# A fused attention and gated-mixing kernel: all eight PSUM banks named by hand, and one written order for all engines

## The chip, the cores and the metric

The kernel runs on one core of a Trainium2 chip. The metric is the device time of one execution in microseconds (us). The core's engines are called by the names of the profile: PE (matrix multiplication, with PEld for its weight loads), DVE (vector work), ACT (activation functions and copies), POOL and SP (here they mostly issue transfers).

## The reference, cut to what matters

Four batches (B = 4) with eight heads (H = 8), a sequence of 768 and a head size of 64. First an attention in which a query sees the 96 keys up to itself and the first 8 keys, with a bias that grows with distance; then a gated mixing over tokens and channels.

```python
scores = scale * np.matmul(q, k.transpose(0, 1, 3, 2)) + bias     # bias = -slope[h] * distance
scores = np.where(is_global | is_local, scores, -1e9)
a = softmax(scores)
x = np.matmul(a, v)                        # to (B, 768, 512): heads side by side
theta = x @ w_theta
zr, zi = x * np.cos(theta), x * np.sin(theta)
y = einsum('ts,bsd->btd', w_tok_r, zr) + einsum('ts,bsd->btd', w_tok_i, zi)
u = x + y
out = u + np.maximum(u @ w_ch, 0.0)
```

## The kernel before, in words

Everything is cut into blocks of 128 tokens (NT = 6 of them) and pairs of heads (NP = 4). All matmuls take bf16. One batch goes through these steps:

- **q and k turned.** q and k of a head pair must lie with the head size on the partitions. Batch 0 is turned by 12 PE transposes of half width (`turn`, L221), batches 1 and 2 by 6 PE transposes (`prep`, L267) of a copy that DVE regroups (`prep_copy`, L252), batch 3 by DMA transposes on SP (`prep_dma`, L284). Copies bring the turned blocks out of PSUM (L232, L271, L273), and `kglob` (L241, L243) makes the copy of k whose first 8 columns are the global keys.
- **Scores.** `score_mms` (L325) makes a chunk of two token blocks for both heads of a pair: 8 matmuls (6 in the last chunk of three), each with 64 rows, the head size, and 128 columns. The two heads use the two halves of the PE array. In batch 0 the bias is first laid into PSUM by matmuls (`score_bias`, L298 and L305); in the others `score_exp` (L335) takes the exponential on ACT and DVE multiplies by a table (L344, L347), which `bias_table` (L148) made per head.
- **Values.** `values` (L387) makes 22 matmuls of 65 columns for a pair, the last column being the softmax sum; DVE divides (L392, L394). `xtrans` turns the result for the next product, by PE transposes (L405, L406) or by DMA transposes (L398).
- **Theta and sines.** `theta` (L428): 24 matmuls of 512 columns for a batch; `sines` on ACT (L438); DVE multiplies (L442) into `zri`.
- **Mix and channels.** `mix` (L453): for each of 6 token blocks 12 matmuls of 512 columns, in three groups of 4, then an addition on DVE (L458). `utrans` turns u, by PE and ACT (L471, L472) or by a DMA transpose (L467). `chan` (L481): 4 matmuls of 512 columns, a DVE instruction (L486) and the store (L488).
- **Token weights.** `trans_w` (L185 to L189) turns the token-mixing weights once, in 72 PE transposes.

PSUM is given out by two pools: `big`, two tiles of two banks each, for scores, values of batches 1 to 3 and theta; and `small`, four tiles of one bank, for all else. A pool hands out its tiles in turn.

The order has three parts. Up to `manual.close()`, batch 0's attention, its theta and its first mixes, the written order of the calls is the order of all engines. Then a loop over batches describes batch b's mix (`main`) and batch b+1's attention (`attention_steps`, as `side`), `weave` interleaves the two by weights, and the tile framework's scheduler makes the engines' queues from it, helped by some anchors (`behind`). The last four calls are in a manual order again, for PE and DVE. Loads go through POOL's queue in the order of `load_w` and what follows it.

```python
    big = ctx.enter_context(tc.tile_pool(name="big", bufs=2, space=bass.MemoryType.PSUM))
    small = ctx.enter_context(tc.tile_pool(name="small", bufs=4, space=bass.MemoryType.PSUM))
```

Of the kernel before, what the change touches and what calls it, by code (L numbers as in the profile page):

```python
# [16 lines left out]
def kernel(  # L17
# [32 lines left out]
    big = ctx.enter_context(tc.tile_pool(name="big", bufs=2, space=bass.MemoryType.PSUM))  # L50
    small = ctx.enter_context(tc.tile_pool(name="small", bufs=4, space=bass.MemoryType.PSUM))

    def ps_big():
        return big.tile([T, 2, 512], FP, name="pb", tag="pb")

    def ps_small(shape, dtype):
        return small.tile(shape, dtype, name="ps", tag="ps")


# [3 lines left out]
    def alloc_qk(b):  # L63
        loads[b] = [ld.tile([T, 2, H, NT, D], BF, name="qk"), None]

    def alloc_v(b):
        vn = loads[b][1] = ld.tile([T, H, NT, D + 1], BF, name="vn")
        nc.vector.memset(vn[:, :, :, D:D + 1], 1.0)
# [38 lines left out]
    alloc_v(0)  # L107
    load_qk(0, 2, 2)
# [51 lines left out]
    def load_w():  # L160
        def tok(tt, wis=(0, 1)):
            for wi, src in [(w_, (moe_w_tok_r, moe_w_tok_i)[w_]) for w_ in wis]:
                w2 = moe.tile([T, 2, S], BF, name="w_nat", bufs=6)
                nc.gpsimd.dma_start(
                    out=w2, in_=src[tt * T:(tt + 2) * T, :].rearrange("(a p) s -> p a s", p=T))
                w_nat[wi, tt], w_nat[wi, tt + 1] = w2[:, 0], w2[:, 1]
        def wth(lo, hi):
            nc.gpsimd.dma_start(out=w_theta_bf[:, lo:hi], in_=moe_w_theta.rearrange("(c p) n -> p c n", p=T)[:, lo:hi])
        tok(0)
        wth(0, 2)  # L170
        wth(2, 4)
        tok(2)
        load_all_qk(1)
        tok(4)
        nc.gpsimd.dma_start(out=w_ch_bf, in_=moe_w_ch.rearrange("(c p) n -> p c n", p=T))
        load_all_v(1)
        load_all_qk(2)

    def trans_w(tt, copy=nc.vector.tensor_copy, wide=False, copy0=nc.vector.tensor_copy):
        pb = big.tile([T, 2, 2 * 512], BF, name="pbw", tag="pb") if wide else None  # L180
        tiles = [pb[:, wi, 0:S].rearrange("p (t n) -> p t n", t=NT) if wide else ps_small([T, NT, T], BF)
                 for wi in range(2)]
        for wi, ps in enumerate(tiles):
            for st in range(NT):
                nc.tensor.transpose(ps[:, st, :], w_nat[wi, tt][:, st * T:(st + 1) * T], ident)  # L185
            if not wide:
                (copy if wi else copy0)(out=w_tokT[wi][:, :, tt * T:(tt + 1) * T], in_=ps)
        for wi, ps in enumerate(tiles if wide else ()):
            (copy if wi else copy0)(out=w_tokT[wi][:, :, tt * T:(tt + 1) * T], in_=ps)  # L189


    def warm(n):
        ps = ps_small([T, 512], FP)
        for _ in range(n):
            nc.tensor.matmul(ps, lhsT=zero[:, 0:T], rhs=zero, start=True, stop=True)


    x_sb, xT_sb = {}, {}
    qkT = {}

    anchor = {}

    def alloc_x(b):
        x_sb[b] = moe.tile([T, NP, NT, T], BF, name="x_sb", bufs=2)
        xT_sb[b] = moe.tile([T, NC, S], BF, name="xT", bufs=1)

    def behind(eng):

        return tc.issue_after(anchor[eng]) if eng in anchor else nullcontext()

    tiles0 = {}

    qk0 = att.tile([T, 2, 2, NT, D], BF, name="qk0", tag="qkn", bufs=2)

    def cast0(i_, eng, h):
        eng(out=qk0[:, i_, h], in_=qk32[:, i_, h])

    def turn(ps, src):
        for t_ in range(NT):
            for hh in range(2):  # L220
                nc.tensor.transpose(ps[hh * D:(hh + 1) * D, t_, :], src[:, hh, t_, :], ident)  # L221

    def turn0(p, i_):
        ps = tiles0[p, i_] = ps_small([T, NT, T], BF)
        turn(ps, loads[0][0][:, i_, 2 * p:2 * p + 2] if p else qk0[:, i_])

    def out0(p, i_, copy, half=None):
        to = qkT.setdefault((0, p), [None, None, None])
        if to[i_] is None:
            to[i_] = att.tile([T, S], BF, name=("qT", "kT")[i_], tag=("qT", "kT")[i_], bufs=6)  # L230
        ns = slice(0, T) if half is None else slice(half * T // 2, (half + 1) * T // 2)
        copy(out=to[i_].rearrange("p (n t) -> p n t", t=NT)[:, ns],  # L232
             in_=tiles0[p, i_].rearrange("p t n -> p n t")[:, ns])

    def kglob(b, p, t0=0, t1=NT - 2, copy=nc.vector.tensor_copy):
        kT = qkT[(b, p)][1]
        if t0 == 0:
            qkT[(b, p)][2] = att.tile([T, NT - 2, T], BF, name="kG", bufs=6)
        kG = qkT[(b, p)][2][:, t0:t1]
        with behind("zri" if p else "dve") if b == B - 1 else nullcontext():  # L240
            copy(  # L241
                out=kG, in_=kT[:, (t0 + 1) * T:(t1 + 1) * T].rearrange("p (t n) -> p t n", t=t1 - t0))
            copy(out=kG[:, :, 0:NG], in_=kT[:, None, 0:NG].to_broadcast([T, t1 - t0, NG]))  # L243

    qkns = {}

    def prep_copy(b, p):
        qk = loads[b][0]
        qkn = qkns[b, p] = att.tile([T, NT, 2, 2, D], BF, name="qkn", bufs=2)
        with behind("dve"):  # L250
            for i_ in range(2):
                nc.vector.tensor_copy(  # L252
                    out=qkn[:, :, i_].rearrange("p t h d -> p h t d"), in_=qk[:, i_, 2 * p:2 * p + 2])

    def prep(b, p):
        if p == 0 or (b, p) == (2, NP // 2):
            prep_copy(b, p)
        if p + 1 < NP and (b, p) != (2, NP // 2 - 1):
            prep_copy(b, p + 1)
        qkn = qkns[b, p]  # L260
        qT = att.tile([T, S], BF, name="qT", bufs=6)
        kT = att.tile([T, S], BF, name="kT", bufs=6)
        for i_, dst in ((0, qT), (1, kT)):
            ps = ps_small([T, NT, T], BF)
            with behind("pe"):
                for t_ in range(NT):
                    nc.tensor.transpose(ps[:, t_, :], qkn[:, t_, i_].rearrange("p h d -> p (h d)"), ident)  # L267
            dst = dst.rearrange("p (n t) -> p n t", t=NT)
            src = ps.rearrange("p t n -> p n t")
            if i_ == 0:  # L270
                nc.vector.tensor_copy(out=dst, in_=src)  # L271
            else:
                nc.scalar.copy(out=dst, in_=src)  # L273

        qkT[(b, p)] = [qT, kT, None]
        kglob(b, p)

    def prep_dma(b, p):
        qk = loads[b][0]
        qkT[(b, p)] = [None, None, None]  # L280
        for i_ in (1, 0):
            to = qkT[(b, p)][i_] = att.tile([T, S], BF, name=("qT", "kT")[i_], bufs=6)
            with behind("sp"):
                nc.sync.dma_start_transpose(  # L284
                    out=to.rearrange("p (t s) -> p t s", t=NT),
                    in_=qk[:, i_, 2 * p:2 * p + 2].rearrange("p h t d -> p (h t d)"))

    ebuf = {}

    pbs = {}  # L290

    def score_bias(p, c):
        pb = pbs[0, p, c] = ps_big()
        n = min(4, 2 * NT - 1 - 4 * c)
# [14 lines left out]
    def score_mms(b, p, c):  # L309
        qT, kT, kG = qkT[(b, p)]  # L310
        if c == 0:
            ebuf[(b, p)] = att.tile([T, 2, NT, 2, T], BF, name="e", bufs=3)
        if b:
            pbs[b, p, c] = ps_big()
        pb = pbs[b, p, c]
# [12 lines left out]
    def sine_table():  # L328
        nc.scalar.activation(junk, halfpi, AF.Sin)

    def score_exp(b, p, c):
        e_t, pb = ebuf[(b, p)], pbs[b, p, c]
        n = min(4, 2 * NT - 1 - 4 * c) * T
        e_c = e_t[:, :, 2 * c:2 * c + 2].rearrange("p a j s n -> p a (j s n)")[:, :, 0:n]
        ins = nc.scalar.activation(e_c, pb[:, :, 0:n], AF.Exp, scale=scale).ins  # L335
        if b and c == NT // 2 - 1 and p == NP - 1:
            with tc.issue_after(ins):
                sine_table()
        if b == 0:
            return  # L340
        tab = etab[:, 2 * p:2 * p + 2]
        if c == 0 or n < 4 * T:
            s0 = 0 if c == 0 else 2
            nc.vector.tensor_mul(e_c, e_c, tab[:, :, s0:s0 + n // T].rearrange("p a s n -> p a (s n)"))  # L344
        else:
            e4 = e_t[:, :, 2 * c:2 * c + 2].rearrange("p a j s n -> p a j (s n)")
            nc.vector.tensor_mul(  # L347
# [20 lines left out]
    def values(b, p, hh, i0=0, i1=NT):  # L368
# [20 lines left out]
        if b and hh == 0:  # L389
            return  # L390
# [348 lines left out]
```

## Time and profile before

| | us |
|---|---|
| median of 3 runs (lowest, highest) | 171.81 (171.68, 172.01) |
| the profiled execution's own time | 171.37 |
| its span, first to last instruction | 169.3 |
| PE, PEld busy | 158.8, 85.1 |
| DVE, ACT, POOL busy | 126.7, 104.6, 38.8 |

The profiled execution took 2.07 us more than its span: what lies before the first and behind the last instruction. Its own time is 0.44 us under the median of the runs.

By stages, with the first theta matmul of each batch as borders (a table by windows of the trace; busy us):

| window | what PE does in it | length | PE | DVE | ACT |
|---|---|---|---|---|---|
| 0 to 8.31 | warm-up, bias, first transposes | 8.31 | 5.77 | 5.80 | 4.64 |
| 8.31 to 24.28 | attention of batch 0 | 15.97 | 15.07 | 11.21 | 14.42 |
| 24.28 to 66.93 | theta and mix of 0, attention of 1 | 42.65 | 41.26 | 37.07 | 35.11 |
| 66.93 to 104.23 | theta and mix of 1, attention of 2 | 37.30 | 35.94 | 32.87 | 24.00 |
| 104.23 to 137.17 | theta and mix of 2, attention of 3 | 32.94 | 32.56 | 25.61 | 19.63 |
| 137.17 to 165.40 | theta and mix of 3, channels | 28.23 | 28.03 | 13.46 | 6.77 |
| 165.40 to 169.30 | last DVE instructions and stores | 3.90 | 0.15 | 0.67 | 0.00 |

How to read it: matmuls are pipelined, and the profile models their ends, so PE can show as busy while nothing enters it. Starts are exact. So the distance from one start to the next tells what a matmul costs in a stream.

### The profile page before, as it was taken

How to read it: one execution, taken by the hardware profiler on the slowest of the kernel's cores; microseconds unless marked ns; L12 is line 12 of the kernel's file. 1: busy time of each engine (PE TensorE's matmuls, PEld its weight loads, DVE VectorE, ACT ScalarE, POOL GpSimd, SP SyncE). 2: the span in 40 equal slices, each digit the busy share in tenths (PEclk: the TensorE clock that was granted, in tenths of full speed). 3: DMA queues.
4: the chain of work that ended last, by engine and by line, in shares of the span. 5: the costliest groups of instructions: out<-in, count | busy, mean ns of one | idle time of the engine just before them, and what ended most of it. 6: DMA issues, size and time to landing. Idle time of an engine off the chain costs nothing.

```text
span 169.3 us, 3778 instructions
## 1 busy us (share of the span) xinstructions
PE 158.8 (94%) x1546; PEld 85.1 (50%) x1569; DVE 126.7 (75%) x265; ACT 104.6 (62%) x134; POOL 38.8 (23%) x46
## 2 busy tenths in 40 slices
PE   7689989999989999999989999999999999999991
PEld 2346755557655455545545464444555544444440
DVE  6748877699999997989998697787877837614442
ACT  4698898995599694799842641999257109400010
POOL 8975439005164101049700000000000000000000
PEclk9999999999999999999999999999999999999999
DMA  5999999999999999709999895776137472233335
GB/s 152 204 172 180 209 206 205 203 209 180 152 202 220 149 172 162 146 6 200 137 125 127 211 166 135 134 149 217 35 77 143 111 170 96 95 62 93 93 96 183
DMA packets 72704, 25.34 MB, mean 150 GB/s; under 512 B 60784, under 2 KB 69744, under 8 KB 72688
## 3 DMA queue, kind: packets, MB, share of 16 engines
q0 software_dynamic: 45696, 12.45, 87.8%
q1 hardware_dynamic: 26576, 12.13, 32.5%
q10 hardware_dynamic: 416, 0.52, 0.9%
q8 instruction: 12, 0.20, 0.5%
q14 instruction: 4, 0.03, 0.1%
HBM read 25.69 MB, written 6.29 MB: 189 GB/s over the span
## 4 chain that ended last, share of the span: by engine, by line
PE 64%; DVE 16%; ACT 11%; DMA 4%; issue 2%; DVEq 0%; SPq 0%
PE ps L453 27%; PE ps L481 9%; PE pb L428 6%; PE pb L325 5%; ACT cs L438 4%; ACT e L335 4%; PE pb L387 4%; PE ps L428 3%; DMA qk<-in_k_dram 3%; PE ps L267 2%; DVE x_sb L394 2%; DVE e L344 2%; DMA xT<-x_sb 2%; PE ps L405 2%; DVE e L347 2%
## 5 line engine op out<-in xcount | busy, mean ns | idle before, releaser
L453 PE MATMUL ps<-zri,w_tokT 128*128 128x512 bf16 x272 | 67.8, 380 | 0.8 <-issue 0.2
L335 ACT ACTIVATE e<-pb 128x1024 bf16<-128x1024 f32 (+1 forms) x48 | 43.6, 955 | 16.6 <-PE pb L325 16.1
L453 PEld LDWEIGHTS <-w_tokT 128*128 128x128 bf16 x288 | 25.8, 98 | 27.3 <-DVE w_tokT L189 0.6
L458 DVE TENSOR_TENSOR u<-x_sb,ps 128x512 bf16<-128x512 bf16 x24 | 16.4, 684 | 13.3 <-PE ps L453 12.9
L481 PE MATMUL ps<-w_ch_bf,uT 128*128 128x512 bf16 (+1 forms) x96 | 23.9, 370 | 0.2
L442 DVE TENSOR_TENSOR zri<-x_sb,cs 128x1024 bf16<-128x1024 bf16 (+1 forms) x30 | 16.6, 581 | 4.9 <-ACT cs L438 4.6
L486 DVE SCALAR_TENSOR_TENSOR o_sb<-ps,u 128x512 f32<-128x512 f32 (+1 forms) x25 | 16.4, 664 | 4.4 <-PE ps L481 4.4
L325 PE MATMUL pb<-qT,kT 64*128 64x128 bf16 x224 | 15.4, 219 | 2.2 <-DVE x_sb L394 0.9
L344 DVE TENSOR_TENSOR e<-e,etab 128x1024 bf16<-128x1024 bf16 (+1 forms) x24 | 14.8, 620 | 2.3 <-ACT e L335 2.2
L325 PEld LDWEIGHTS <-kT 64*128 64x128 bf16 x224 | 8.8, 94 | 14.4 <-issue 10.3
L472 ACT COPY uT<-ps 128x512 bf16<-128x512 bf16 x7 | 4.2, 597 | 18.9 <-PE ps L471 18.9
L438 ACT ACTIVATE cs<-pb,halfpi 128x1024 bf16<-128x1024 f32 x8 | 8.9, 1114 | 10.7 <-PE pb L428 10.6
L428 PE MATMUL pb<-w_theta_bf,xT 128*128 128x512 bf16 x62 | 15.0, 379 | 0.2
L387 PEld LDWEIGHTS <-e 128*128 128x128 bf16 x352 | 12.7, 97 | 3.7 <-issue 1.2
L481 PEld LDWEIGHTS <-uT 128*128 128x128 bf16 x100 | 9.2, 98 | 9.9 <-ACT uT L472 0.8
L428 PEld LDWEIGHTS <-xT 128*128 128x128 bf16 x96 | 8.9, 98 | 10.0 <-DMA xT<-x_sb 0.6
L88 POOL DMA_DIRECT2D vn<-in_v_dram x5 | 9.6, 1916 | 11.4 <-DVE qkn L252 10.2
L325 PE MATMUL pb<-qT,kG 64*128 64x128 bf16 x128 | 11.8, 216 | 0.1
L394 DVE TENSOR_TENSOR x_sb<-pb,rec 128x768 bf16<-128x768 f32 x12 | 11.5, 958 | 0.4
L347 DVE TENSOR_TENSOR e<-e,etab 128x1024 bf16<-128x1024 bf16 x12 | 8.3, 689 | 2.9 <-ACT e L335 2.8
L387 PE MATMUL pb<-vn,e 128*128 128x65 bf16 x168 | 9.6, 193 | 0.3 <-DVE e L344 0.2
L273 ACT COPY kT<-ps 128x768 bf16<-128x768 bf16 x8 | 6.3, 800 | 5.2 <-PE ps L267 5.1
(81 smaller groups left out, 213.0 us busy)
## 6 DMA issues: line engine op xcount, KB each, us to landing
out_dram<-o_sb SPq DMA_DIRECT2D x23, 256.0 KB, 2.3
vn<-in_v_dram POOLq DMA_DIRECT2D x3, 768.0 KB, 23.1
qk<-in_q_dram POOLq DMA_DIRECT2D x2, 768.0 KB, 20.6
qk<-in_k_dram POOLq DMA_DIRECT2D x2, 768.0 KB, 22.2
w_nat<-in_moe_w_tok_r_dram POOLq DMA_DIRECT2D x3, 384.0 KB, 13.0
w_nat<-in_moe_w_tok_i_dram POOLq DMA_DIRECT2D x3, 384.0 KB, 14.1
vn<-in_v_dram POOLq DMA_DIRECT2D x2, 384.0 KB, 10.4
qk<-in_q_dram POOLq DMA_DIRECT2D x8, 96.0 KB, 9.8
```

The lines of the kernel that those rows point to most:

```text
L325: nc.tensor.matmul(pb[:, hh, o:o + T], lhsT=lhsT, rhs=qT[R, (own, nxt)[part]], start=bool(b), stop=bool(b) or (jt == NT - 1 or (j == 1 and ...
L335: ins = nc.scalar.activation(e_c, pb[:, :, 0:n], AF.Exp, scale=scale).ins
L344: nc.vector.tensor_mul(e_c, e_c, tab[:, :, s0:s0 + n // T].rearrange("p a s n -> p a (s n)"))
L387: nc.tensor.matmul(po4[:, head - h0, it - i0], lhsT=l_, rhs=r_, start=(i_ == 0), stop=(i_ == len(mms) - 1))
L394: nc.vector.tensor_mul(xv, po4[:, :, :, 0:D], rec.to_broadcast([T, n, nt, D]))
L428: nc.tensor.matmul(pb[j_] if last else pb[:, j_, :], lhsT=xT[:, dc, st(j_)], rhs=w_theta_bf[:, dc, :], start=(dc == 0), stop=(dc == NC - 1))
L438: nc.scalar.activation(o, p_, AF.Sin, **bias)
L442: anchor["zri"] = nc.vector.tensor_mul(zri[b][:, i_, 2 * c + j_:2 * c + j_ + n, :].rearrange("p j (g d) -> p j g d", g=NP), xb[:, :, 2 * c ...
L453: anchor["pe"] = nc.tensor.matmul(ps, lhsT=w_tokT[wi][:, st, tt * T:(tt + 1) * T], rhs=zri[b][:, wi, st, :], start=(st == 0 and wi == 0), ...
L458: anchor["dve"] = nc.vector.tensor_add(u_sb[b, tt].rearrange("p (g d) -> p g d", g=NP), x_sb[b][:, :, tt, :], ps.rearrange("p (g d) -> p g ...
L481: nc.tensor.matmul(ps_c, lhsT=uT[:, dc, :], rhs=w_ch_bf[:, dc, i_ * n:(i_ + 1) * n], start=(dc == 0), stop=(dc == NC - 1))
L486: nc.vector.scalar_tensor_tensor(o_sb[:, cols], in0=ps_c, scalar=0.0, in1=u[:, cols], op0=ALU.max, op1=ALU.add)
```

## The change

PSUM becomes one tile of eight banks. Each accumulator takes the next number of a written list (`banks`), or that bank and the next where it needs two; so any bank may hold anything. All calls become small steps ("ops"), and one list, `order`, of 660 steps for all four batches is executed in a manual order for every engine: the weaving, the scheduler's part and the anchors are gone. Step names: `q` transposes q (0) or k (1), `qe` copies them out, `pc` regroups, `pd` is the DMA transpose, `kg` the global keys, `sb` the bias, `s`, `e`, `x` scores, exponential and table product, `v`, `n` values and division, `xt`, `xe`, `xd` the turning of x by PE or DMA, `th`, `sn`, `z` theta, sines and products, `m`, `u` mix and addition, `ut`, `ue`, `ud` the turning of u, `c`, `r`, `st` channels, result and store, `w`, `we` token weights, `bt` a bias table, `l...` loads. Arguments are batch, head pair or token block, chunk; `a` or `v` names ACT or DVE.

In `v` the two heads of a pair take turns token block by token block, where one head came after the other. Some copies change engine. The buffers of `e`, `u`, `uT` and others keep their number.

```diff
-    big = ctx.enter_context(tc.tile_pool(name="big", bufs=2, space=bass.MemoryType.PSUM))
-    small = ctx.enter_context(tc.tile_pool(name="small", bufs=4, space=bass.MemoryType.PSUM))
+    psum = ctx.enter_context(tc.tile_pool(name="psum", bufs=1, space=bass.MemoryType.PSUM))
+    bank = psum.tile([T, 8, 512], FP, name="bank")
+    banks = []
     def ps_big():
-        return big.tile([T, 2, 512], FP, name="pb", tag="pb")
+        i_ = banks.pop(0)
+        return bank[:, i_:i_ + 2, :]
     def ps_small(shape, dtype):
-        return small.tile(shape, dtype, name="ps", tag="ps")
+        ps = bank[:, banks.pop(0), :]
...
+    @op
+    def s_(b, p, c):
+        qT, kT, kG = qkT[b, p]
+        if b:
+            ps_of["s", b, p, c] = ps_big()
+        pb = ps_of["s", b, p, c]
...
+    @op
+    def v_(b, p, hh, i0, i1):
...
+        for it in range(i0, i1):
+            for head in range(h0, h0 + n):
...
+    @op
+    def xd_(b, p):
+        nc.sync.dma_start_transpose(
+            out=xT_of(b)[:, p, :].rearrange("p (t s) -> p t s", t=NT),
+            in_=x_sb[b][:, p].rearrange("p t d -> p (t d)"))
...
-    load_w()
-    alloc_x(0)
...
-        weave(main, side, 0.1 if b == 0 else 0.0, 0.9)
...
+    order = """
+        warm.1.3 diag.2 warm.6.0 dist diag.0 bt.6 diag.1 sb.0.1 cast.1.1.a cast.0.0.v warm.3.1 bt.0
+        cast.0.1.a diag.3 cast.1.0.v bt.4 q.0.1.0 q.0.0.0 qe.0.1.0.v.2 q.0.0.1 qe.0.0.0.a.0
+        qe.0.0.1.a.0 qe.0.0.0.a.1 q.0.1.1 kg.0.0.0.1.v qe.0.0.1.v.1 lw.0 sb.0.0 qe.0.1.1.a.2 swap
+        s.0.0.0 kg.0.0.1.4.a sb.0.2 kg.0.1.0.4.v q.0.2.0 lt.0.2 e.0.0.0 q.0.2.1 qe.0.2.0.v.2 lt.2.4
...
+        xt.0.3.4.6 xe.0.3.2.4.v bt.2 xe.0.2.0.6.v th.0.0.4 lv.1.0.8 we.0.1.v we.0.0.v th.0.0.5
+        th.0.0.3 th.0.1.2 sn.0.0.0 lq.2.0.8 sn.0.0.1 w.2.0 z.0.0.0 th.0.1.3 xe.0.3.4.6.v w.2.1
+        sn.0.1.0 z.0.0.1 th.0.2.2 mv.2 sn.0.1.1 we.1.1.v m.0.1.0 we.2.0.v sin.0 z.0.1.1 th.0.2.3
...
+        u.0.1 w.4.0 pc.1.2.0 ut.0.0 kg.1.0.0.4.v we.4.0.a m.0.2.2 qe.1.1.1.v.2 ue.0.0.a s.1.0.1
+        pc.1.2.1 s.1.0.0 s.1.0.2 kg.1.1.0.4.v e.1.0.0 m.0.2.1 pc.1.3.1 lq.3.0.4 e.1.0.2 q.1.3.1
...
+        x.1.2.0 xd.1.1 pc.2.0.0 s.1.2.2 u.0.4 s.1.3.1 e.1.2.2 s.1.3.2 st.0.0.2 m.0.5.2 pc.2.0.1
...
+        q.2.1.0 m.0.5.1 qe.2.1.0.a.2 xe.1.2.0.6.v q.2.1.1 qe.2.0.1.a.2 r.0.3.2 xt.1.3.0.6 th.1.0.0
...
+        v.3.3.2.0.6 c.2.0.2 n.3.1.2.0.6 xd.3.2 m.2.5.0 n.3.3.2.0.6 xd.3.1 c.2.2.2 m.2.4.1 ud.2.1
+        m.2.5.1 u.2.4 xd.3.3 th.3.0.0 th.3.1.0 st.1.4.2 th.3.0.6 ud.2.3 m.2.5.2 ud.2.4 th.3.0.3
...
+        r.3.2.2 c.3.3.2 st.3.2.2 u.3.5 c.3.1.2 r.3.3.2 ut.3.5 r.3.1.2 c.3.4.2 ue.3.5.a st.3.1.2
+        c.3.5.1 r.3.4.2 st.3.3.2 c.3.5.0 r.3.5.1 st.3.4.2 r.3.5.0 st.3.5.1 st.3.5.0
+    """
+    banks += [int(i_) for i_ in "".join("""
+        760545324632430247632067420706327654376140620456327410635401620532510526024063202546024603
...
+    for word in order.split():
+        name, *args = word.split(".")
+        do(name, *(int(a_) if a_.isdigit() else a_ for a_ in args))
     manual.close()
```

## The prediction

> **What bounds the kernel now.** I read the page's busy times and its chain first, then what PE waits for, then rows of the timeline from start to start, because a busy PE is not yet a full one.
>
> ```profile
> PE 158.8 (94%) x1546; PEld 85.1 (50%) x1569; DVE 126.7 (75%) x265; ACT 104.6 (62%) x134; POOL 38.8 (23%) x46
> ...
> PE 64%; DVE 16%; ACT 11%; DMA 4%; issue 2%; DVEq 0%; SPq 0%
> ```
>
> PE is busy for 94% of the span and holds 64% of the chain that ended last. No other engine is near. The list of PE's waits names little:
>
> ```profile
> PE ps L195 <- DVE zero L105: 1.2, 1, 1.2
> PE pb L325 <- DVE x_sb L394: 0.9, 1, 0.9
> PE pb L325 <- DVE qT L232: 0.7, 1, 0.7
> PE ps L221 <- DVE qk L216: 0.7, 1, 0.7
> ```
>
> Three of these four lie before 8.4 us. So what can a new order win on PE? That needs the price of a matmul in a stream. From the timeline (start, busy, engine and line, operation, count):
>
> ```profile
> 159.88 2.75 PE L453 MATMUL ps<-zri,w_tokT 128*128 128x512 bf16 x12
> ...
> 162.47 1.03 PE L481 MATMUL ps<-w_ch_bf,uT 128*128 128x512 bf16 x4
> ```
>
> Twelve matmuls of 512 columns take 162.47 - 159.88 = 2.59 us from start to start, 0.216 each. Now the scores between them:
>
> ```profile
> 115.75 0.34 PE L325 MATMUL pb<-qT,kT 64*128 64x128 bf16 x6
> 115.93 0.22 PE L325 MATMUL pb<-qT,kG 64*128 64x128 bf16 x2
> 116.08 1.04 PE L453 MATMUL ps<-zri,w_tokT 128*128 128x512 bf16 x4
> 117.05 0.23 PE L325 MATMUL pb<-qT,kT 64*128 64x128 bf16 x2
> ...
> 117.39 0.22 PE L325 MATMUL pb<-qT,kT 64*128 64x128 bf16 x2
> 117.55 1.04 PE L453 MATMUL ps<-zri,w_tokT 128*128 128x512 bf16 x4
> ```
>
> Eight score matmuls take 116.08 - 115.75 = 0.33 us, fourteen take 117.55 - 117.05 = 0.50: the six more cost 0.17, about 0.03 each, so 0.09 of the 0.33 is not for the eight. And the four mix matmuls at 116.08 take 0.97 until the next scores start, where 4 x 0.216 = 0.86: another 0.1. So **each change between the tile shapes 128\*128 and 64\*128 costs PE about 0.09 us**, with nothing waiting. Over all such places the medians are 0.096 in and 0.092 out; I take 0.092.
>
> Then PE's own time without stalls, in program order: 494 matmuls of 512 columns (288 mix, 96 theta, 92 channels, 8 bias, 10 warm-up) x 0.216 = 106.6; 238 full transposes x 0.056 = 13.3; 352 scores x 0.030 = 10.6; 352 value matmuls x 0.029 = 10.2; 96 half transposes x 0.028 = 2.7; the short rest 2.8: together 146.2. The queue of the kernel before changes its tile shape 82 times: 7.5. From PE's first start at 1.20 that would end at 154.9; the last matmul starts at 165.28. So **stalls are about 10.4 us**: 3.4 before 8.31, 1.8 up to theta at 24.28, 2.7 in the stage to 66.93, 1.4 to 104.23, 0.7 to 137.17, 0.4 behind it. Behind PE's end 3.9 us remain.
>
> **The change, part by part.**
>
> *Fewer changes of shape.* PE's 1569 matmuls are the same in kind and number. The list puts score chunks side by side (for example s.1.0.1, s.1.0.0, s.1.0.2 follow each other on PE, and all of pair 0 lies in one visit). Any two of the eight banks can hold a chunk, so three chunks can be open where `big` had two tiles. Counted in the built queue, the shape changes 50 times instead of 82: 24 instead of 32 before the first theta, then 10 instead of 22, 8 instead of 14, 8 instead of 14. 32 x 0.092 = **2.9 us less**, all on PE's path.
>
> By the Trainium skill, "TensorEngine Tiling (Array Packing)", Key Properties, changing the tiling mode drains the TensorE; the rows above agree and give the price. The page gives none; "TensorE: Matmul & The Clock Gate", Step-by-step, puts the drain at about 128 cycles, 0.053 us at its 2.4 GHz: by that estimate the gain would be 1.7 us, and the measured rows decide.
>
> *The head, up to theta.* Casts cannot start before q and k land (5.01 and 5.31 us). New is that ACT makes two more bias tables (bt.0, bt.4, 0.72 each) between and behind its casts, and turns pair 1 first (its q lands at 6.18). By hand: cast.0.1 ends near 6.8 instead of 6.0, q.0.0.0 and q.0.0.1 run to 7.5, three half copies on ACT (0.48 each) to 8.9, the last on DVE to 9.4: first scores near 9.5 instead of 8.31, 1.1 later. But by then pair 1's first copies (0.80 and 0.96) and the tables are done. ACT then needs twelve exponentials, which follow each other at 0.92 and 0.75, plus two copies: about 12, from 10.4 to 22.5. Then come the last values, division and transposes, 1.3: theta near 24, and w_theta's second half lands at 24.56 in any case, since POOL's loads keep their order. I take theta at 24.4, as before. What is gained is that all values and transposes of x and the second block of token weights stand before it: about 1.5 us of PE work that before lay behind 24.28 (0.34 transposes of x, 0.5 values, 0.67 token weights).
>
> *From theta to the end.* PE's sums with the changes of shape, by stage of the new list: 38.6 (24 theta, 72 mix and 16 channel matmuls are 24.2; 148 transposes 8.3; scores and values 5.2; 10 changes 0.9), 32.3, 31.0 and 30.5, together 132.4. With theta at 24.4 PE would end at 156.8 without a stall; before it was 165.4.
>
> *What stalls remain* is the unknown. Below: the order is fixed so that no wait of more than a hand-over stays, 1.3 us in all four stages. Above: DVE. In the stage after theta its rows add up to 39.0 (12 table products 7.7, 4 divisions 4.7, 5 additions 3.4, 3 results 2.1, z 5.0, 13 regroupings 4.7, token weights 4.4, the rest 7.0), or 36.2 if they overlap as all DVE rows do (rows 136.7, busy 126.7), against PE's 38.6. Before, DVE was busy 37.07 of 42.65, 87%. At 87%, 36.2 needs 41.6: stalls of 3.0. In the next stage 32.2 or 29.9 against 32.3; at 88% as before, 33.9: 1.6 at most. After that DVE has room (25.5 of 31.0, 17.3 of 30.5). I take 4.3 for all, a little less than the 5.2 of before: some 2.6 in the first stage, 0.9, and 0.8 for the last two.
>
> *Values by turns.* The two heads' matmuls now alternate between two banks. No row shows that for L387; the nearest is L325, which alternates so and costs nothing for it. Bounds: 0, and one change's 0.09 for each of 12 pairs, 1.1. I take 0.
>
> *Moved copies.* Five copies of k's global keys go from DVE to ACT (0.6 each), two turned u to DVE; DVE is about 2.4 us lighter, ACT about 2 heavier, and ACT has 34 of 38.6 in its fullest stage: nothing on the path. The tables of `bt` no longer stand in a burst of seven (5 us); ACT had time there, nothing. The sine table loads (1.28) stand before the first sine and wait for no matmul: hidden in ACT's idle time before theta's first chunk, else 1.28 per batch.
>
> *Queues.* SP is now in one order: xd.1.1 is issued 7.6 us of PE work before th.1.0.0, which has to wait for it. Before, two such transposes among the loads landed 7.8 and 8.2 us after issue. So 0.6 at most, contained in the 0.9; the rest of PE's queue stands behind it. The loads of batch 2 land at 51.7 and 56.3, and pc.2.0.0 and pc.2.0.1 come on DVE at about 55.7 and 57.3: late enough; if they slip by 2 us, DVE's stores of results and PE's transposes behind it do too. The DMA transposes of k and q of batch 3 wait on SP for heads that land behind the gate, with ud behind them; u is needed only much later.
>
> *PSUM itself.* In the built queues every wait for a bank names the last reader of that same bank; one tile for all does not tie the banks together. So naming them costs nothing.
>
> **Sum.** 24.4 + 132.4 + 4.3 = 161.1 for PE's end, + 3.9 behind it (the last channel steps are the same) = span 165.0, + 2.1 around it = 167.1 against 171.37 of the profiled execution. The median lies 0.4 above that execution: **167.5 against 171.81**.
>
> **The rivals.**
>
> *Dense.* Nearly no stalls: 1.3 instead of 4.3, so 164.5. For it: from 137 us on PE already runs with 0.4 of stalls. Against: DVE's 36 to 39 beside PE's 38.6.
>
> *Given back.* The changes of shape go, but the denser PE meets later partners: stalls grow from 5.2 to 7 or 8, so 170 to 171.5. For it: 2.7 us of stalls are there today with more cover.
>
> *DVE becomes the bound: slower.* A fixed order lets one late DVE instruction hold all behind it. If DVE's rows do not overlap (39.0 and 32.2) and it keeps its idle share, the stages take 39.0 / 0.87 = 44.8 and 32.2 / 0.88 = 36.6: 6.2 and 4.3 of stalls, with 1.1 behind and theta at 24.6: 3.2 + 4.3 = 7.5 over the forecast, 175.0. It decides from 8.6 us of stalls behind theta: there the time is that of before. For it: DVE is busy for 9.93 of the 10 us from 80 to 90 even now. Against: it is 2.4 us lighter in all.
>
> That one tile couples the banks would be a fourth, but the queues exclude it.
>
> **How the numbers follow.** Forecast (165.5 to 169.5) 0.53, dense 0.20, given back 0.11, slower 0.16. The range goes from the dense case to a little above the time before, with half of the slower case: 164.3 to 172.5. Faster by over 0.2% (what a measurement can tell from no change): 0.53 + 0.20 + 0.08 = 0.81; within, 0.03; slower, 0.16.
>
> **What would show it.** Right: the first theta near 24.4, the second near 65.5, the last PE start near 161; score matmuls in visits of 14 or more. Wrong: PE idle before L325's successor with DVE named in the stage to 66 us; first scores after 10 us with theta later than 25.5; th.1 held by a DMA.

## The result and the profile after

The changed kernel takes **170.14 us** (median of 4 runs, 169.76 to 170.48) against 171.82 (171.68 to 172.01) of the kernel before in the same comparison: a ratio of 0.990, interval 0.988 to 0.993. So it is faster by 1.7 us, 1%; 4.3 us had been forecast. Its profiled execution took 170.19 us with a span of 168.1.

Of the experiments below, two runs each of e2 and e7, one each of e8 and e9, three of e11 and four of e12 show a mean PE clock of 0.984 to 0.990 and are 1 to 3 us longer than the others of their kernel; the medians below hold them, the ratios leave out about half of them, and "at full clock" means without them.

The page's busy times and the shares of the chain that ended last, of the kernel after:

```profile
PE 154.2 (92%) x1547; PEld 86.2 (51%) x1569; DVE 124.8 (74%) x257; ACT 106.6 (63%) x142; POOL 38.5 (23%) x46
...
PE 59%; DMA 18%; DVE 15%; issue 2%; SPq 2%; ACT 1%; POOL 0%; DVEq 0%; POOLq 0%
```

PE is busy 4.6 us less and holds 59% of the chain instead of 64%. DMA holds 18% where it held 4%: more than four times the share. What PE waits for (engine and line, releaser: us in all, times, longest):

```profile
PE bank L477 <- DMA xT<-x_sb: 2.7, 2, 1.6
PE bank L550 <- DVE u L519: 1.6, 1, 1.6
...
PE bank L550 <- DMA uT<-u: 0.7, 1, 0.7
```

Before, theta (L477 here) and the channels (L550 here) were in none of the lines shown; now these lines make up 5.0 us. A visit of scores to PE, in the timeline from start to start:

```profile
116.17 0.34 PE L362 MATMUL bank<-qT,kT 64*128 64x128 bf16 x6
...
116.80 0.22 PE L362 MATMUL bank<-qT,kG 64*128 64x128 bf16 x2
116.95 1.04 PE L511 MATMUL bank<-zri,w_tokT 128*128 128x512 bf16 x4
```

24 score matmuls take 116.95 - 116.17 = 0.78 us: 24 x 0.029 and one change of shape, 0.09. Before, 14 of them took 0.50. The rows by stage (length; busy us of PE, PEld, DVE, ACT, POOL; clock; DMA share; GB/s), the borders again being the first theta of each batch, and at the end the last PE start:

```profile
24.58:63.35 38.77, 38.30 (x431) 24.21 (x437) 34.55 (x77) 32.78 (x45) 12.14 (x11) 1.00 1.84 188
63.35:100.08 36.73, 32.33 (x323) 17.87 (x327) 30.11 (x55) 24.16 (x33) 10.29 (x11) 1.00 1.64 132
100.08:133.31 33.23, 30.88 (x290) 16.01 (x293) 23.64 (x41) 22.50 (x28) 0.00 (x0) 1.00 0.47 107
133.31:163.73 30.42, 30.26 (x145) 13.97 (x147) 15.65 (x25) 6.77 (x9) 0.00 (x0) 1.00 0.50 133
```

Priced as in the prediction (each matmul at its price in a stream, 0.092 per change of shape), PE's work and what is left over as stalls is (estimates; of the kernel before, the first theta matmul of batch 2 starts at 104.07, where the table of stages had 104.23):

| stage | before: length = work + stalls | after: length = work + stalls |
|---|---|---|
| theta of 0 to theta of 1 | 42.64 = 39.98 + 2.66 | 38.77 = 38.53 + 0.25 |
| theta of 1 to theta of 2 | 37.14 = 35.61 + 1.54 | 36.73 = 32.43 + 4.30 |
| theta of 2 to theta of 3 | 33.10 = 32.38 + 0.73 | 33.23 = 30.96 + 2.27 |
| theta of 3 to PE's last start | 28.11 = 27.75 + 0.37 | 30.42 = 30.12 + 0.30 |

The first stage is 3.9 us shorter and almost without a stall. The next two hold 4.6 us less work and 4.3 us more of stalls. Only 1.1 of the 4.6 is saved, by 12 fewer changes of shape; twenty transposes (1.1) now lie in front of the first theta or in the first stage, and twelve matmuls of 512 columns lie in the last stage, which has 2.4 us more work for it and is 2.3 us longer. Six places make up 6.4 of the 7.1 us of stalls: 1.74 at theta of batch 1 (63.35), 0.51 and 0.46 at 81 and 85, 1.51 at 91.28, 1.29 at theta of batch 2 (100.08), 0.90 at 106.78. The chain that ended last shows what stands behind three of them, at 63.35, 91.28 and 106.78 (start, us, what); at 100.08 it is a DMA transpose of x again, by the list above:

```profile
55.59 9.44 DMA xT<-x_sb
...
65.30 1.67 PE bank L477 x7
...
81.91 10.14 DMA kT<-qk
92.07 0.30 DVE kG L322
...
102.12 2.76 DMA kT<-qk
...
105.41 2.44 DMA uT<-u
...
107.90 1.04 PE bank L550 x4
```

Two DMA transposes took 9.44 and 10.14 us from issue to landing; the two later ones, like all but one behind 100 us, 2.4 to 2.8. In the flight of the slow ones a 768 KB load of values through POOL was on its way: batch 2's landed at 65.91, batch 3's was issued at 79.44 and landed at 95.09. Loads of 96 KB of q and k were on their way too, until 70.73 and until 83.99. What the second one does to PE is seen in rows of the timeline:

```profile
92.07 0.29 DVE L322 COPY kG<-kT 128x512 bf16<-128x512 bf16 x1 [2.23 <-DMA kT<-qk]
...
92.48 0.68 DVE L519 TENSOR_TENSOR u<-x_sb,bank 128x512 bf16<-128x512 bf16 x1
...
93.22 1.02 PE L550 MATMUL bank<-w_ch_bf,uT 128*128 128x512 bf16 x4 [1.56 <-DVE u L519]
```

DVE waits 2.23 us in line for batch 3's k, which no score needs before 110 us. Behind it stands the addition u.1.3, and PE's channel matmul (c.1.1) waits for that, though it does not read its result: its own turned u landed at 84.30. It waits for its bank. By the two lists c.1.1 gets bank 7, which m.1.3 filled and u.1.3 has still to read. The two banks of s.2.3.0 had been read by 90.67, before PE came to c.1.1 at 91.7, but they are given to the next values. No run here gives c.1.1 another bank; so late transpose, order on DVE and choice of bank share this stall. In the kernel before, batch 3's first transpose of k was issued at 95.64, when its load of values had landed (92.24), and took 3.3 us.

### The profile page after: what moved, and what is told of

The parts are those of the page before. It is cut to its first block, busy times and chain, and to the rows that moved or that the text cites. A ratio compares the mean times of both kernels' runs of the same rounds, so it can differ in the third digit from the quotient of the medians.

```text
span 168.1 us, 3796 instructions
## 1 busy us (share of the span) xinstructions
PE 154.2 (92%) x1547; PEld 86.2 (51%) x1569; DVE 124.8 (74%) x257; ACT 106.6 (63%) x142; POOL 38.5 (23%) x46
## 4 chain that ended last, share of the span: by engine, by line
PE 59%; DMA 18%; DVE 15%; issue 2%; SPq 2%; ACT 1%; POOL 0%; DVEq 0%; POOLq 0%
PE bank L511 27%; PE bank L477 9%; PE bank L550 9%; DMA kT<-qk 8%; DMA xT<-x_sb 6%; PE bank L362 4%; PE bank L421 4%; DMA qk<-in_q_dram 3%; DVE e L383 2%; DVE x_sb L434 2%; DVE kT L299 2%; PE bank L265 2%; SPq L312 1%; DMA uT<-u 1%; DVE kG L322 1%
## 5 line engine op out<-in xcount | busy, mean ns | idle before, releaser
L511 PE MATMUL bank<-zri,w_tokT 128*128 128x512 bf16 x273 | 66.8, 379 | 1.4 <-issue 1.0
L374 ACT ACTIVATE e<-bank 128x1024 bf16<-128x1024 f32 (+1 forms) x48 | 42.9, 955 | 8.9 <-PE bank L362 8.3
L550 PE MATMUL bank<-w_ch_bf,uT 128*128 128x512 bf16 (+1 forms) x98 | 24.1, 370 | 2.4 <-DVE u L519 1.6
L477 PE MATMUL bank<-w_theta_bf,xT 128*128 128x512 bf16 x92 | 22.8, 379 | 2.9 <-DMA xT<-x_sb 2.7
L519 DVE TENSOR_TENSOR u<-x_sb,bank 128x512 bf16<-128x512 bf16 x24 | 16.2, 684 | 11.2 <-PE bank L511 11.0
L558 DVE SCALAR_TENSOR_TENSOR o<-bank,u 128x512 f32<-128x512 f32 (+1 forms) x25 | 16.2, 666 | 7.9 <-PE bank L550 7.5
L434 DVE TENSOR_TENSOR x_sb<-bank,rec 128x768 bf16<-128x768 f32 (+2 forms) x21 | 16.1, 767 | 0.7
L550 PEld LDWEIGHTS <-uT 128*128 128x128 bf16 x100 | 9.3, 98 | 12.3 <-issue 1.8
L477 PEld LDWEIGHTS <-xT 128*128 128x128 bf16 x96 | 8.8, 97 | 13.0 <-DMA xT<-x_sb 3.9
L362 PE MATMUL bank<-qT,kT 64*128 64x128 bf16 x224 | 12.9, 218 | 0.4 <-DVE qT L299 0.3
L421 PE MATMUL bank<-vn,e 128*128 128x65 bf16 x224 | 13.2, 193 | 0.1
L362 PE MATMUL bank<-qT,kG 64*128 64x128 bf16 x128 | 10.7, 216 | 0.0
```

The costliest lines, as they stand in the source:

```text
L362: nc.tensor.matmul(pb[:, hh, o:o + T], lhsT=lhsT, rhs=qT[R, (own, nxt)[part]], start=bool(b), stop=bool(b) or (jt == NT - 1 or (j == 1 and ...
L374: nc.scalar.activation(e_c, ps_of["s", b, p, c][:, :, 0:blocks(c) * T], AF.Exp, scale=scale)
L421: nc.tensor.matmul(po4[:, head - h0, it - i0], lhsT=l_, rhs=r_, start=(i_ == 0), stop=(i_ == len(mms) - 1))
L434: nc.vector.tensor_mul(xv, po4[:, :, :, 0:D], rec.to_broadcast([T, m_, nt, D]))
L477: nc.tensor.matmul(ps_of["th", b, c][j_], lhsT=xT_sb[b][:, dc, (2 * c + j_) * T:(2 * c + j_ + 1) * T], rhs=w_theta_bf[:, dc, :], start=(dc ...
L511: nc.tensor.matmul(ps_of["m", b, tt], lhsT=w_tokT[wi][:, st, tt * T:(tt + 1) * T], rhs=zri[b][:, wi, st, :], start=(mixed[b, tt] == 0), st ...
```

## The experiments

Theory A: the missing gain is lost where DMA transposes land late and an engine waits for them in its fixed order; A1, because a large load is in flight; A2, because of SP's own order. Theory B: the order is so dense that, whichever wait is taken away, the next partner is as late. In the diffs the words of `order` that matter are shown; a bank number moves with its step.

**e1: theta of batch 1 takes its head pairs in the order 0, 2, 1, 3**, so that the late transpose (pair 1) is needed third.

```diff
-        for j_, dc in part:
+        pairs = (0, 2, 1, 3) if b == 1 else range(NC)
+        for j_, at in part:
+            dc = pairs[at]
...
-        xt.1.3.0.6 th.1.0.0 u.0.5 kg.2.0.0.4.a th.1.1.0 r.0.2.2 xe.1.3.0.6.a th.1.0.6
+        xt.1.3.0.6 th.1.0.4 u.0.5 kg.2.0.0.4.a th.1.1.4 r.0.2.2 xe.1.3.0.6.a th.1.0.5
```

> Batch 1's theta takes the head pairs in the order 0, 2, 1, 3, and 8 matmuls that need only pairs 0 and 2 come first, so that pair 1, whose DMA transpose landed at 65.03 in the changed kernel, is asked for 1.7 us later. Theory A (the missing gain was lost to DMA transposes that land 8 to 10 us after their issue, with PE or DVE waiting in line): the stall of 1.74 us at 63.35 shrinks to 0.3 and the time falls by 1.2 to 1.5 us from 170.1, to about 168.8. Theory B (the written order is dense, and any wait that goes is replaced by the next partner, DVE or ACT): the stall goes, but batch 1's sines or z take its place and the time falls by less than 0.4 us.

Measured: 167.3 us (166.53 to 167.85), ratio 0.974 (0.970 to 0.978): 2.8 us less than the changed kernel, about twice what A expected. The timeline of e1 shows theta running through:

```profile
63.21 2.39 PE L479 MATMUL bank<-w_theta_bf,xT 128*128 128x512 bf16 x9
65.44 0.39 PE L537 MATMUL bank<-ident,u 128*128 128x128 bf16 x4
```

That wait was real loss, and 1.1 us more went with it than it measured: in e1 PE reaches the channels of batch 1 with no stall there, k's transpose landing at 89.08, and the 0.90 us at 106.78 are gone too. The wait at theta of batch 2 grew, from 1.29 to 2.03. So A for this wait, with a little of B.

**e2: DVE's copy of the late k (kg.3.2) moved behind kg.3.3**; **e3: e1 and e2 together.**

```diff
-        m.1.5.1 kg.3.2.0.4.v st.0.5.2
+        m.1.5.1 st.0.5.2
...
-        kg.3.3.0.4.v th.2.0.3
+        kg.3.3.0.4.v kg.3.2.0.4.v th.2.0.3
```

> The copy of the global keys for pair 2 of batch 3 (kg.3.2), for which DVE waited 2.2 us until a DMA transpose landed at 92.05, stands 14 us later on DVE, behind kg.3.3; its reader, s.3.2.0, comes at 111. Theory A: the 1.5 us for which PE waited behind it (c.1.1 for a bank that DVE had not read) go, the divisions of batch 2 come earlier, so do the transposes of x that theta of batch 2 waited 1.3 us for: 1.5 to 2.8 us less, 167.3 to 168.6. Theory B: DVE has 30 of 37 us of work in that stage and something else on it is late: less than 0.4 us.

> Both of the edits before (theta order of batch 1, later kg.3.2). Theory A: the gains add, 2.7 to 4.3 us less than 170.1, so 165.8 to 167.4. Theory B: less than 0.8 us together.

Measured: e2 169.15 (168.12 to 170.44; at full clock 168.12 and 168.32), ratio 0.985 (0.979 to 0.992); e3 167.56 (166.7 to 168.15), 0.975 (0.972 to 0.979). In e2's trace the 1.5 us at 91 are gone, the stalls of that stage are 2.68 instead of 4.30, but theta of batch 2 waits 1.78. At full clock e2 is 1.9 us faster than the changed kernel, as A expected. But A's sum for e3 (165.8 to 167.4) did not come: two waits in one chain do not add up, and e3 is no faster than e1, which had removed this wait already.

**e5: batch 3's values loaded only behind the products of theta 2** (its wait on POOL, gt.2.0, with it).

```diff
-        m.1.2.0 lv.3.0.8 pc.2.3.1
+        m.1.2.0 pc.2.3.1
...
-        z.2.0.0 sin.3
+        z.2.0.0 gt.2.0 lv.3.0.8 sin.3
...
-        e.3.0.0 vg.3.0.8 s.3.0.2
+        e.3.0.0 s.3.0.2
...
-        x.3.2.0 v.3.0.2.0.6
+        x.3.2.0 vg.3.0.8 v.3.0.2.0.6
```

> Only the load of v for batch 3 is changed: it waits on POOL until the first z of batch 2 (some 105 us) instead of starting at 79.4, where it moved until 95.1; its reader vg.3 moves behind it on DVE, to just before the first values of batch 3. If the transposes of 80 to 95 us are late because that load shares the DMA engines (theory A1), they land some 2.8 us after issue instead of 6 to 10, DVE's wait for kg.3.2 goes and the time falls by 1.5 to 2.8 us. If they are late because of their own order on SP's queue (theory A2), their times to landing stay and so does the time. Should the load come too late, values of batch 3 wait for it near 120 us, up to 2 us.

Measured: 169.7 (169.4 to 169.94), ratio 0.988 (0.986 to 0.990). The transfers issued from 78 to 92 us (median us to landing in the last column), first in the kernel after, then in e5:

```profile
vn<-in_v_dram POOLq DMA_DIRECT2D x1, 768.0 KB, 15.7
uT<-u SPq DMA_TRANSPOSE x3, 5.2
kT<-qk SPq DMA_TRANSPOSE x2, 9.2
```

```profile
uT<-u SPq DMA_TRANSPOSE x3, 4.7
kT<-qk SPq DMA_TRANSPOSE x2, 3.2
```

SP's order is the same, the load is gone, and k lands in 3.2 us instead of 9.2: that is A1, shown for batch 3's transposes. For xT at 55.59 no run moved the load in its flight; there the cause is taken over from here. The stalls of that stage fall from 4.30 to 1.61. Some 1.0 of this is not the transposes: the stalls of 0.51 and 0.46 are gone as well, and they stand behind a copy on DVE that POOL's issue of this load held up (e10 and e12 below). The time falls hardly at all, because the values now come late (landing at 118.10) and PE waits for their copy, as the expectation had allowed for:

```profile
PE bank L477 <- DMA xT<-x_sb: 2.9, 2, 1.8
PE bank L421 <- DVE vG L398: 1.6, 1, 1.6
```

**e4: eleven PE steps put back into the visits of scores**, so that the shape changes 72 times instead of 50 (for example):

```diff
-        s.3.1.2 s.3.3.0 e.3.1.2 s.3.1.1 x.3.2.1 m.2.3.0
+        s.3.1.2 s.3.3.0 m.2.3.0 e.3.1.2 s.3.1.1 x.3.2.1
```

> The changed kernel with 11 PE steps (ten groups of mix matmuls and one set of weight transposes) moved into the middle of visits of score matmuls in batches 1 and 3: PE's tile shape changes 72 times instead of 50, and nothing else changes. If a change costs 0.092 us on PE's path: 1.1 us more in the stage after the first theta (12 changes), 0.9 more in the one after theta of batch 2 (10 changes), from start to start; of the first, up to 1.1 may be hidden by the wait for the DMA transpose at theta of batch 1, which does not move if DVE keeps its pace. So 1 to 2 us more than 170.1. If the gap at a change is hidden or is only a feature of how starts are recorded: no change.

Measured: 172.83 (170.34 to 173.76, ten runs), ratio 1.001 (0.996 to 1.005). The median is 2.7 us above the changed kernel's, but the runs scatter by 3.4; the ratio, which leaves out the four longest, is 1.6 to 1.8 us above that of the changed kernel (0.990, and 0.991 in e8), against 22 x 0.092 = 2.0. In the trace the stage from theta 2 to theta 3 has ten more changes, 0.92 by that price, and took 33.97 us instead of 33.23, with 0.3 us less of waits for DMA transposes. In the first stage moved mixes made 1.5 us of new stalls as well, so the whole cannot be read as the price; it agrees with it.

**e6: batch 2's theta in the order 0, 3, 2, 1 as well**, with the ACT copy of pair 3 moved ahead; **e7: e6 without the gate** (`gt.1.2`, a POOL instruction that holds the loads of batch 3 until a product of batch 1 is there); **e8: the changed kernel once more**.

```diff
-        pairs = (0, 2, 1, 3) if b == 1 else range(NC)
+        pairs = {1: (0, 2, 1, 3), 2: (0, 3, 2, 1)}.get(b, range(NC))
...
-        xt.2.3.0.6 u.1.4 th.2.0.0 st.0.4.2 xe.2.3.0.6.a
+        xt.2.3.0.6 xe.2.3.0.6.a u.1.4 th.2.0.4 st.0.4.2
```

> The theta order of batch 1 (0, 2, 1, 3; alone it gave 167.3) and in the same way batch 2's (0, 3, 2, 1), so that pairs 2 and 1, whose DMA transposes landed last, are asked for about 1.5 us later. Alone with batch 1's edit PE waited 2.0 us at 97.1 for them. Theory A: this stall falls to 0.5 or less, 165.5 to 166.3. Theory B: less than 0.4 us below 167.3.

> As the kernel with both theta orders, and POOL no longer waits for z of batch 1 before the last loads of batch 3 (gt.1.2 left out): the second half of q and k and v of batch 3 start near 70 instead of 73 and 79, so v lands near 90.5 instead of 94.5. Theory A1 (loads in flight make the transposes late): the transposes of 85 to 97 us land sooner by some us, and what is left of the waits for them goes; 0 to 1.0 us less than the kernel with the gate. Against it: transposes of u at 76 to 80 us, if they meet the same load, are late all the same, and their readers come later. Theory A2 (SP's own order): no change.

> The changed kernel unaltered, beside the two that follow on the same chip. 169.8 to 170.5 us as before. If the landing of the DMA transposes decides its time (theory A), its runs scatter more than those of the kernel before, since the stalls depend on where the loads stand; with theory B they scatter alike.

Measured: e6 168.26 (166.35 to 168.93), ratio 0.977 (0.970 to 0.984); e7 167.98 (167.04 to 168.54), 0.980 (0.976 to 0.984); e8 170.43 (169.65 to 172.83), 0.991 (0.989 to 0.994). e6 has no gain over e1: theta of batch 2 waits 0.62 instead of 2.03, but 1.28 are new at a channel step that waits for a transpose of u. Here B is right: the partner behind is as late. e7 decides nothing between A1 and A2: its 0.3 us less than e6 lie within the scatter. e8 confirms the result, and its trace has the same six stalls (1.72, 0.51, 0.46, 1.33, 1.18, 0.71). At full clock its runs scatter by 1.7 us, those of the kernel before beside it by 0.8, which A expected.

**e9: e7 with the transposes in the order in which they are needed** (kg.3.2 as in e2, ud.1.3 first, the channels of block 3 ahead of block 5); **e10: the same with the gate.**

```diff
-        m.1.4.2 pd.3.0.1 r.1.0.2
+        m.1.4.2 ud.1.3 pd.3.0.1 r.1.0.2
...
-        z.2.0.1 c.1.5.2 pd.3.2.0
+        z.2.0.1 c.1.3.2 pd.3.2.0
```

> Both theta orders, no gate, kg.3.2 behind kg.3.3 on DVE, and of the channel steps of batch 1 block 3 before block 5, with its transpose issued on SP before those of batch 3's k, so that no matmul asks for a transpose in the first 5 us after its issue. In the kernel with both theta orders and no gate PE still waited 0.9 us at 89.5 (behind kg.3.2) and 1.1 at 103.5 (transpose of u). Theory A: both go, 165.5 to 166.5 us. Theory B: they are replaced, above 167.3.

> The same with the gate left in. Theory A: within 0.5 us of the one without the gate, since no reader stands close behind its transpose any more. Theory B: above 167.3.

Measured: e9 166.41 (165.77 to 168.54), ratio 0.966 (0.964 to 0.968); e10 168.17 (167.81 to 168.67), 0.978 (0.976 to 0.980). e9 is as A expected; that the gate costs 1.8 us was not foreseen. The rows of e10 show a part of it, on DVE and then on POOL:

```profile
79.25 2.10 DVE L306 COPY qkn<-qk 128x768 bf16<-128x768 bf16 x1
```

```profile
78.88 2.29 POOL L92 DMA_DIRECT2D vn<-in_v_dram  x1
```

The copy takes 0.35 us at most other places. Here it begins while POOL issues the load of values and ends 0.18 us behind POOL's end. In e5, where that load is issued later, the copy at the same place (80.32) takes 0.35. The kernel after has the same (1.88 us at 80.03, POOL from 79.44 to 81.72): the stalls of 0.51 and 0.46 at 81 and 85 stand behind this copy. The kernel before had it too, in a copy of global keys (1.79 us instead of 0.29, at 81.97), which no transpose waited for. By the Trainium skill, "SBUF — State Buffer", Who interferes with whom, a DVE copy in a two-port mode and a GpSimd instruction (POOL's) exclude each other for the whole of the one that came first. The rows agree with that, though none shows the mode of the copy; a table product of DVE with two inputs that began just ahead of POOL (0.68 us at 78.65) was not held.

**e11: e9 with DVE's kg.3.3 and kg.3.2 behind the products of theta 2; e12: e10 with that copy (pc.2.3.1) ahead of the gate.**

```diff
-        kg.3.3.0.4.v kg.3.2.0.4.v th.2.0.3
+        th.2.0.3
...
-        z.2.2.1 s.3.0.0
+        z.2.2.1 kg.3.3.0.4.v kg.3.2.0.4.v s.3.0.0
```

```diff
-        c.0.4.2 gt.1.2 sn.1.2.1
+        c.0.4.2 pc.2.3.1 gt.1.2 sn.1.2.1
...
-        lv.3.0.8 pc.2.3.1 pd.3.0.0
+        lv.3.0.8 pd.3.0.0
```

> The kernel of e9 with one change: kg.3.3 and kg.3.2 on DVE moved behind the last product of batch 2, z.2.2.1. In e9 the product z.2.0.1 (L500) started 1.33 us late at 104.15 because DVE waited 4.58 us at kg.3.3 for the DMA transpose of k, and PE waited 1.62 at the first mix matmul of batch 2 (105.50). Theory A (a late transpose with an engine waiting in line): nearly all of that wait goes, 1.2 to 1.6 us less than e9, 164.8 to 165.2. Theory B (the next partner is late instead): at most 0.4 less, 166.0 to 166.4.

> The kernel of e10 (all shifts, gate kept) with one change: the second half of pc.2.3, a copy of 128x768 by DVE, moved in front of the gate gt.1.2. Why e10 lost 1.8 us against e9, which has no gate, was not foreseen. Theory A3: the gate puts POOL's issue of the load of batch 3's v (78.88 to 81.17) beside this copy (79.25), which then takes 2.10 us instead of 0.35, and PE waits 0.73 for it and 0.46 for the copies behind it. If so, the copy takes 0.35 at its new place and the time falls by 0.7 to 1.2 us, to 167.0 to 167.5. If the copy is slow for another reason, or if the gate costs by the later landing of the loads themselves, the time stays within 0.3 of 168.2.

Measured: e11 167.51 (166.09 to 169.05), ratio 0.972 (0.967 to 0.976); at full clock 166.09 to 166.73, as e9. So A's step fell: DVE's copies were not what came last. e12: 169.6 (167.15 to 170.28), ratio 0.983 (0.978 to 0.988); at full clock 167.15 and 167.38, where e10 took 167.81 to 168.67. In the trace the copy takes its normal time,

```profile
71.69 0.34 DVE L306 COPY qkn<-qk 128x768 bf16<-128x768 bf16 x1
```

the stage from theta 1 to theta 2 falls from 33.92 to 32.83 us and the span from 166.1 to 164.9; the stalls of 0.73 and 0.46 behind the copy are gone. So the held copy cost this order some 1.2 us, shown in the trace; by the medians over all runs it cannot be seen. For the wait that e11 left, the chain of e9 has the answer:

```profile
97.11 2.80 DMA kT<-qk
...
99.93 0.63 ACT kG L322
...
100.80 1.28 ACT L491
...
102.09 2.04 ACT cs L491 x2
...
104.76 0.69 DVE zri L500
...
105.50 1.90 PE bank L513 x8
```

Another copy of global keys, kg.3.0, stands on ACT ahead of the sines: ACT waits for the transpose, and the table load, the sines, the products and PE follow.

**e13: e9 with kg.3.0 on ACT behind the sines; e14: e12 with the same.**

```diff
-        th.2.1.4 kg.3.0.0.4.a th.2.0.5
+        th.2.1.4 th.2.0.5
...
-        sn.2.2.0 pd.3.3.0
+        sn.2.2.0 kg.3.0.0.4.a pd.3.3.0
```

> The kernel of e9 with one change: kg.3.0 on ACT moved from in front of the first sine of batch 2 to behind sn.2.2.0. Theory A in the form the trace of e11 suggests (ACT waits in line for the late transpose of k, and the sines, DVE's products and PE's first mix matmul of batch 2 stand behind it): ACT's table load starts near 98.8 instead of 100.80, PE's wait of 1.62 at the first mix matmul falls under 0.5, the time by 1.0 to 1.8 us, to 164.6 to 165.4. If DVE's own two copies (kg.3.3, kg.3.2, still in front of the products and ready at 102.6) hold the line as well, the gain is 1.0 to 1.2 instead of 1.8. Theory B (dense order, the next partner is as late): 166.0 to 166.4.

> The kernel of e12 (gate kept, copy in front of the gate) with the same change, kg.3.0 on ACT behind sn.2.2.0. Theory A: the wait of 2.1 us at the first mix matmul of batch 2 falls under 0.6, the profiled span from 164.9 to 163.1 to 163.8, and the time of runs at the full clock from 167.2 to 165.4 to 166.0. If the clock that some runs lose (0.984 to 0.990 in the mean) follows from that very gap in PE's work, as in the trace of e11, all runs here keep a clock above 0.994. Theory B: span 164.5 or more.

Measured: **e13 165.22** (164.91 to 166.66), ratio 0.963 (0.960 to 0.966), the fastest here; e14 166.25 (166.13 to 166.85), 0.969 (0.967 to 0.971), a little above the 165.4 to 166.0 expected. ACT's table load starts at 97.96 instead of 100.80, and PE's largest wait behind 20 us in e13 is this:

```profile
PE bank L513 <- DVE zri L500: 0.7, 1, 0.7
```

A holds: the medians of e9 and e13 differ by 1.2 us, the ratios by 0.6, and this wait fell from 1.62 to 0.74; e14 is 1.0 us below e12 at full clock. The forecast under 0.5 for this wait missed a little (0.7), as DVE's copies still hold it. With the gate (e14) it is 1.0 us slower even now, though the held copy is gone. The two traces do not show where, since e13's profiled execution, 166.66, was the longest of its six. That stays open.

## Why the prediction missed

*What held.* 50 changes of shape instead of 82: e4 agrees with the price, and PE's sum of work behind theta, 132.4 forecast, is 132.0. Theta of batch 0 at 24.58 (24.4 forecast). One tile for all banks ties nothing together: of the long waits behind theta one is for a bank, and it names the reader of that same bank. But "naming them costs nothing" was too strong: the stall at 91.28 is a wait for bank 7, which the list gave to c.1.1 while u.1.3 had still to read it. Behind PE's last start lie 4.4 us instead of 3.9; the 3.9 was counted from 165.40, and from the last start before (165.28) it was 4.0.

*What failed is the term for the stalls, 4.3, and in it the paragraph on queues: "So 0.6 at most, contained in the 0.9."* Measured behind theta: 7.1. By stage it was wrong in both directions. For the first stage 2.6 was taken, from DVE's idle share; DVE is busy 34.55 of 38.77 us, 89%, and the stall was 0.25: a busy share says little about waits when the order is fixed. For the second 0.9 was taken, and for the last two 0.8: measured 4.30 and 2.57. That the total is off by only 2.8 is in part luck, as 2.3 too much in the first stage makes up for some of the 5.2 too little behind it. Adding up: 0.2 for theta, -0.4 for the work, 2.8 for the stalls and 0.5 behind PE's end give the 3.1 us by which the profiled execution exceeded the 167.1 forecast for it.

The failed step had three parts. First, xd.1.1 was seen with 7.6 us of work ahead of its reader, and two transposes of 7.8 and 8.2 us were known; but this one took 9.44, and the wait was 1.74. e1 took it away. ("th.1 held by a DMA" was one of the signs of being wrong that the prediction named.) Second, "the DMA transposes of k and q of batch 3 wait on SP for heads that land behind the gate, with ud behind them; u is needed only much later": u was needed sooner than that once, at 106.78, where PE waited 0.90 us; u.1.5 was ready at 101.23, and its transpose was issued on SP at 105.41, behind two of k, two stores and another u. More was lost otherwise. The list moves these transposes from 95 us, behind the load of values, to 82 us, into its flight, where those of k take 8 to 10 us (e5), and puts copies that wait for them on DVE and ACT ahead of urgent work (e2, e13). I costed the transposes and not the instructions that wait for them, nor what is queued behind those. Third, a copy of 0.35 us was moved beside POOL's 2.3 us of issue (e5, e12).

The rival "given back", stalls of 7 to 8 and 170 to 171.5, is what came, by its number and in the main by its mechanism, later partners, though it did not name them; 0.11 was too little for it, since the trace of before already showed the two slow transposes and the load that landed between them. DVE as the bound did not come.

## What to carry to other kernels

When an order is fixed by hand, look at each instruction that waits for a transfer and ask what stands behind it on its engine: a copy that nobody needs for 20 us can hold an addition that PE needs now. Take a transfer's time from rows with the same traffic around it, not from its median, and place it against the loads in flight. Read the chain back to where a wait begins before choosing which partner to move, and expect two waits of one chain not to add up.

## What the runs showed of the hardware

- In the kernel after, a DMA transpose from SP lands 2.4 to 2.8 us after its issue behind 100 us, with one of 3.8, and 6 to 10 us after it while a 768 KB load from POOL's queue is in flight (issued from 80 to 90 us); those of k there take 10.1 and 8.3, and with that load moved away 3.2 and 3.3 (e5).
- An SBUF-to-SBUF copy of bf16 on DVE went from 0.35 to 2.10 us beside POOL's 2.29 us of issue (e10; 0.34 in e12).
- In the profiled execution of e11 PE had nothing to start for 2.5 us, and then ran at half its clock: windows of 1 us from 105, with the granted clock in the last but two columns.

```profile
105.00:106.00 1.00, 0.00 (x0) 0.00 (x0) 1.00 (x2) 1.00 (x4) 0.00 (x0) 1.00 0.32 63
106.00:107.00 1.00, 0.69 (x2) 0.27 (x3) 1.00 (x3) 1.00 (x4) 0.00 (x0) 0.68 0.89 178
107.00:108.00 1.00, 1.00 (x4) 0.33 (x3) 1.00 (x3) 1.00 (x3) 0.00 (x0) 0.50 1.00 287
108.00:109.00 1.00, 1.00 (x4) 0.43 (x3) 1.00 (x3) 1.00 (x3) 0.00 (x0) 0.50 0.79 148
```

  Eight mix matmuls took 109.68 - 106.31 = 3.37 us instead of 1.73. By the Trainium skill, "TensorE: Matmul & The Clock Gate", What's actually happening, the gate falls back after an idle window of some 3.4 us that runs freely. Here an idle time of 2.5 us was enough in one execution, while in the profiled execution of e12, with 2.1 us idle at the same place, the clock stayed full. Of e13 and e14, where the gap is under 0.8 us, no run was under 0.994. But that the gap is the cause of the longer runs elsewhere is not shown: only one run of each has a trace, and two runs of e7, whose largest idle time behind 20 us is 0.97 us in its trace, were at 0.984 and 0.986.
